# Fused attention and expert layers on one Trainium2 core: K and V of a batch loaded in two transfers each over all 128 partitions, q(0), q(1) and the gate requested by ACT, and K's fifth column turned at a step's end

## The chip, the cores and the metric

The kernel runs on one core of one Trainium2 chip. The metric is the device time of one execution in microseconds (us); lower is better. Times of the kernel before are three runs on one chip; the trace shown further down is one further execution of the same kernel, taken by the hardware profiler. Engines are named as the profile names them: PE is the matrix engine and PEld its weight loads, DVE the vector engine, ACT the scalar engine, POOL GpSimd, and SP the queue that issues most DMAs.

## The reference

Attention over K and V that are averaged in groups of eight rows, then a layer of eight experts with one expert for each token, then a layer with a squared ReLU. Only the attention is touched by the change.

```python
B, H, S, D = 4, 8, 576, 64
k_p = k.reshape(B, H, S // 8, 8, D).mean(axis=3)        # 72 rows for each head
v_p = v.reshape(B, H, S // 8, 8, D).mean(axis=3)
scores = matmul(q, k_p.transpose(0, 1, 3, 2)) / sqrt(D)
attn = softmax(scores)
x = matmul(attn, v_p)                                   # then (2304, 512): one row for each token
logits = x @ w_gate;  expert = argmax(logits);  gate = softmax(logits)[expert]
y[token] = gate * (relu(x @ w1[expert]) @ w2[expert])   # up to `capacity` tokens for each expert
out = (s * relu(y @ w_in) ** 2 + b) @ w_out
```

## The kernel before

The attention comes first and takes about the first 120 us; the experts (up to about 375 us) and the last layer follow, and both keep PE nearly full. The order of the work is written out by hand: each engine runs its instructions in the order in which the Python code emits them, and waits on semaphores where it needs another engine or a transfer.

The attention works on 20 tiles of up to 128 query rows, five for each of the four batches (four of 128 rows and one of 64), with all eight heads in a tile. Step i of the loop turns q of tile i+4 (`turn_q`: four transposes on PE into `tq`, and a copy to `qT` by ACT), makes the scores of tile i+3 (`scores`: PE products into `sc`, then on DVE the row maxima `mx` and the subtraction into `s`, then on ACT two exponentials, `e` and `s`), multiplies tile i by V (`values`: PE into `o`, then DVE into `xr` and the gate's logits `lg`), and turns the weights of tile i+2 (`turn_e`: PE into `te`, and a copy to `eT` by ACT). Tile i=1 gets its values ahead of step 0, so step 1 has none.

Four things have to be ready for a batch b. K is loaded (`load_k`) and its eight rows of a group are added up (`pool_steps`, three additions of 256, 128 and 64 columns for each head) into `kp`; `prep_k` turns `kp` on PE into the bank `misc` and moves it, scaled, into the block-diagonal `kbd`, which every score product of the batch reads. V is loaded (`load_v`), added up in the same way into `vp`, and `prep_v0` and `prep_v1` make `vx` from it. The additions are shared out between DVE and POOL.

K of a batch lies on 72 partitions (one for each pooled row), eight heads side by side, in two transfers of four heads. V of a batch lies on 128 partitions in five columns. A column p below four holds the pair of heads 2p and 2p+1: rows 0 to 71 are the even head's and rows 72 to 127 the first 56 of the odd head. The last 16 rows of the four odd heads stand in the fifth column, at partitions 16 to 31 of each group of 32. V needs six transfers: one of 72 partitions, one of 56, and four of 16.

SP issues all of these transfers and those of q in the order of the code. Eight completion counters are shared by the DMAs that SP and ACT issue, so that the ninth DMA waits until the first has landed, and so on. There is one buffer for K and one for V; q has four.

Of the kernel before, what the change touches and what calls it, by code (L numbers as in the profile page):

```python
# [7 lines left out]
F32 = mybir.dt.float32  # L8
# [4 lines left out]
ALU = mybir.AluOpType  # L13
# [5 lines left out]
B, H, S, D = 4, 8, 576, 64  # L19
# [3 lines left out]
POOL = 8  # L23
SP = S // POOL
P = 128
NB = 5
# [50 lines left out]
def attention(nc, tc, c, a, cap, capp, left, big, xd, run, hist, first, ps0):  # L77
# [3 lines left out]
    with ExitStack() as es:  # L81
# [6 lines left out]
        nc.vector.memset(wg, 0.0)  # L88
        kbd = [one.tile([P, 4, 2 * SP], F32, name=f"kbd{i}") for i in range(2)]
        vx = [one.tile([P, G, VW], F32, name=f"vx{i}") for i in range(2)]  # L90
        vraw = big.tile([P, NB, POOL, D], F32, name="vraw")
        nc.gpsimd.memset(vraw[:, 4], 0.0)
        for i in range(2):
            nc.vector.memset(kbd[i], 0.0)
            nc.gpsimd.tensor_scalar(out=vx[i][:, :, D], in0=c.mask, scalar1=float(POOL), scalar2=None, op0=ALU.mult)
# [26 lines left out]

        raw, sums = {}, {}

        def load_k(b):
            r = big.tile([SP, H, POOL, D], F32, name="kraw")
            src = a["k"][b].rearrange("h (n j) d -> n h j d", j=POOL)
            for i in range(2):
                nc.sync.dma_start(out=r[:, 4 * i:4 * i + 4], in_=src[:, 4 * i:4 * i + 4])
            raw["k", b] = r  # L130

        def load_v(b):
            src = a["v"][b].rearrange("(p w) (n j) d -> w n p j d", w=2, j=POOL)
            nc.sync.dma_start(out=vraw[0:SP, 0:4], in_=src[0])
            nc.sync.dma_start(out=vraw[SP:P, 0:4], in_=src[1, 0:P - SP])
            for p in range(4):
                nc.sync.dma_start(out=vraw[32 * p + 16:32 * p + 32, 4], in_=src[1, P - SP:, p])
            raw["v", b] = vraw

        def pool_steps(kv, b, h0, h1, eng):  # L140

            hs = slice(h0, h1)
            r = raw[kv, b][:, hs]
            if (kv, b) not in sums:
                sums[kv, b] = two.tile([SP, H, D] if kv == "k" else [P, NB, D], F32, name=kv + "p")
# [12 lines left out]
            yield  # L158
            for z in each(few[2]):
                eng.tensor_add(dst[:, z], r[:, z, 0], r[:, z, 1])  # L160
            yield

        def pool_all(kv, b, h0, h1, eng):
            for _ in pool_steps(kv, b, h0, h1, eng):
                pass

        def prep_k(b):
            tp = ps0.tile([P, 4, SP], F32, name="misc")
            for p in range(4):
                nc.tensor.transpose(tp[:, p], sums["k", b][:, 2 * p:2 * p + 2].rearrange("n h d -> n (h d)"), c.ident[:SP, :SP])  # L170
            for w in range(2):
                r = slice(D * w, D * w + D)
                dst = kbd[b % 2][r, :, SP * w:SP * w + SP]
                if b:
                    nc.scalar.mul(dst, tp[r], KSCALE)
                else:
                    nc.vector.tensor_scalar(out=dst, in0=tp[r], scalar1=KSCALE, scalar2=None, op0=ALU.mult)

        vts = {}

# [23 lines left out]
        N = len(tiles)  # L204
        qs, qts, ss, ets = {}, {}, {}, {}

        def load_q(i):
            if i < N:
                b, t = tiles[i]
                n = rows(t)  # L210
                qs[i] = two.tile([P, H, D], F32, name="q", bufs=4)
                nc.sync.dma_start(out=qs[i][:n], in_=a["q"][b, :, t * P:t * P + n].rearrange("h s d -> s h d"))

        def turn_q(i, bank="tq"):
            if i < N:
                n = rows(tiles[i][1])
                q = qs.pop(i)
                tq = ps1.tile([P, 2, 4, P], F32, name="te")[:, 0] if bank == "te" else ps0.tile([P, 4, P], F32, name="tq")
# [38 lines left out]
        def turn_e(i):  # L257
            if i < N:
                n = rows(tiles[i][1])
                s, e = ss.pop(i)  # L260
                te = ps1.tile([P, 2, 4, P], F32, name="te").rearrange("k j p s -> k (j p) s")
                for p in range(4):
                    nc.tensor.transpose(te[:, p, :n], s[:n, p, 0:P], c.ident[:n, :n])
                nc.tensor.transpose(te[:, 4, :n], e[:n].rearrange("s p k -> s (p k)"), c.ident[:n, :n])
                ets[i] = two.tile([P, NB, P], F32, name="eT", bufs=4)
                nc.scalar.copy(ets[i][:, :, :n], te[:, 0:NB, :n])
# [174 lines left out]
            else:  # L441
                nc.vector.tensor_copy(lists, n)

        load_k(0)
        load_gate()
        load_q(0)
        load_q(1)
        load_v(0)
        load_q(2)
        load_q(3)  # L450
        load_k(1)
        pool_all("k", 0, 0, 3, nc.vector)
        pool_all("k", 0, 3, 4, nc.gpsimd)
        pool_all("k", 0, 4, 7, nc.vector)
        pool_all("k", 0, 7, 8, nc.gpsimd)

        first.nc.sync.dma_start(out=first.idc.rearrange("(p n) o -> p (n o)", p=SUB), in_=big_ids)
        o = ps1.tile([P, 2, 512], F32, name="o")
        for _ in range(33):
            nc.tensor.transpose(o[:, 0, 0:P], c.ident, c.ident)  # L460
        turn_q(0)
        prep_k(0)
        turn_q(1, "te")
# [13 lines left out]
        turn_e(1)  # L477
        for i in (4, 5, 6, 7):
            load_q(i)
        load_v(1)  # L480
        pool_all("k", 1, 0, 5, nc.gpsimd)
        pool_all("k", 1, 5, H, nc.vector)
        dv = iter(())
        for i, (b, t) in enumerate(tiles):
            now[0] = i + 1
            if t == 1 and 0 < b < B - 1:
                prep_k(b + 1)
            if t == 3 and 0 < b < B - 1:
                prep_v0(b + 1)
            turn_q(i + 4)  # L490
            if i == 1:
                prep_k(1)
            scores(i + 3)
            if t == 4 and b < B - 1:
                prep_v1(b + 1)
# [7 lines left out]
            if i == 3:  # L503
                prep_v0(1)
            turn_e(i + 2)
            load_q(i + 8)
            if b >= B - 2:
                scale()
# [5 lines left out]
            if b + 1 < B:  # L514
                if t == (b == 0):
                    pool_all("v", b + 1, 0, SPLIT[b], nc.gpsimd)
                    dv = pool_steps("v", b + 1, SPLIT[b], NB, nc.vector)
                    next(dv)
                    if b:
                        next(dv)  # L520
                if i in (1, 4):
                    load_k(2 if i == 1 else 3)
                if t == 3 and b + 2 < B:
                    load_v(b + 2)
                if i in (2, 3):
                    pool_all("k", 2, 4 * i - 8, 4 * i - 4, nc.gpsimd)
                elif i == 6:
                    pool_all("k", 3, 0, 4, nc.gpsimd)
                    pool_all("k", 3, 4, 8, nc.gpsimd)
# [1125 lines left out]
```

## Time and profile before

| | |
|---|---|
| Time of three runs | 633.31, 635.12 and 637.03 us, median 635.12 us |
| The profiled execution | 635.53 us, of which 633.8 us lie between its first and last instruction |
| PE busy | 583.3 us (92% of the span) |
| DVE busy | 371.0 us (59%) |
| ACT busy | 249.4 us (39%) |
| POOL busy | 277.2 us (44%) |
| Moved by DMA | 86.12 MB, mean 136 GB/s |

All times in the trace count from its first instruction. Shares of the whole span say little here, since the attention and the two layers behind it have different limits; the attention is read from its own stretch.

### The profile page before, as it was taken

What the parts mean: (1) busy time and instruction counts of PE and PEld (TensorE: products, weight loads), DVE (VectorE), ACT (ScalarE), POOL (GpSimd) and SP (SyncE); (2) the same over time, 40 slices, a digit from 0 to 9 for tenths busy, and PEclk for the clock granted to TensorE, in tenths of its full rate; (3) what the DMA queues carried; (4) which work ended last, traced back from release to release, by engine and by line L of the source; (5) the groups of instructions that cost most, each with busy time, mean ns of one, the idle gap of its engine ahead of it and who ended that gap; (6) DMA issues with size and microseconds to landing.
All of it is one profiled execution on the core that took longest, in us unless ns stands there. A gap on an engine that the chain in (4) does not pass through costs nothing. (4 is left out here: it accounts for less than half of the span.)

```text
span 633.8 us, 11287 instructions
## 1 busy us (share of the span) xinstructions
PE 583.3 (92%) x4005; PEld 540.7 (85%) x4005; DVE 371.0 (59%) x901; ACT 249.4 (39%) x614; POOL 277.2 (44%) x462
## 2 busy tenths in 40 slices
PE   5788989699899969998899898999999999999995
PEld 5787878689899969998899778889899899899895
DVE  4687898977978976573758999713712022021050
ACT  1354654535456645435325635314115024033040
POOL 6557644715244805213207703406726336156051
PEclk8799999699899989999999998999999999999998
DMA  8999776636748895756677201017300100100000
GB/s 167 191 188 181 164 220 211 208 113 210 264 134 273 271 306 179 259 173 204 196 220 289 78 25 43 2 50 282 113 21 1 51 18 2 50 18 3 19 20 20
DMA packets 67951, 86.12 MB, mean 136 GB/s; under 512 B 24713, under 2 KB 40073, under 8 KB 67856
## 3 DMA queue, kind: packets, MB, share of 16 engines
q1 hardware_dynamic: 57168, 71.04, 38.1%
q10 hardware_dynamic: 8240, 7.14, 3.8%
q0 software_dynamic: 2448, 6.82, 3.4%
q8 instruction: 42, 0.69, 0.5%
q14 instruction: 53, 0.43, 0.2%
HBM read 68.09 MB, written 17.58 MB: 135 GB/s over the span
## 5 line engine op out<-in xcount | busy, mean ns | idle before, releaser
L1442 POOL TENSOR_TENSOR gl<-rt,gh 128x128 fp32r<-128x128 f32 x176 | 87.5, 519 | 84.0 <-ACT gh L1439 79.7
L1449 PE MATMUL bank<-wo,gh 128*128 128x512 f32 (+1 forms) x340 | 99.5, 376 | 0.2 <-DVE wo L1400 0.2
L936 POOL TENSOR_TENSOR w1l<-kraw,w1h 128x128 fp32r<-128x128 f32 x96 | 51.5, 569 | 51.9 <-ACT w1h L929 51.8
L1113 PE MATMUL bank<-hs,w2h 128*128 128x288 f32 (+1 forms) x308 | 68.5, 311 | 5.5 <-issue 5.1
L1449 PEld LDWEIGHTS bank<-wo,gh 128*128 128x128 f32 x340 | 62.0, 188 | 12.8 <-DVE wo L1400 0.5
L1449 PE MATMUL bank<-wo,gl 128*128 128x512 f32 (+1 forms) x170 | 63.8, 375 | 0.0
L1456 DVE SCALAR_TENSOR_TENSOR raw<-bank,sb,c_u 128x512 f32<-128x512 f32 (+1 forms) x14 | 10.0, 711 | 82.1 <-PE bank L1449 82.1
L1113 PEld LDWEIGHTS bank<-hs,w2h 128*128 128x128 f32 x308 | 50.7, 192 | 6.5 <-issue 5.9
L1424 ACT ACTIVATE rt<-tq 128x256 f32<-128x256 f32 (+1 forms) x26 | 9.5, 367 | 110.5 <-PE tq L1040 89.6
L1113 PE MATMUL bank<-hs,w2l 128*128 128x288 f32 (+1 forms) x148 | 44.9, 303 | 0.0
L1439 ACT CAST gh<-rt 128x256 fp32r<-128x256 f32 (+1 forms) x96 | 36.7, 383 | 17.4 <-DVE rt L1425 11.1
L944 POOL DMA_INDIRECT xg<-xd,u_idx x23 | 26.2, 1138 | 33.5 <-DVE r L290 13.9
L1457 POOL DMA_INDIRECT out_dram<-raw,it x12 | 12.5, 1040 | 63.2 <-DVE raw L1456 62.6
L1425 DVE SCALAR_TENSOR_TENSOR rt<-bank,rt 128x256 f32<-128x256 f32 (+1 forms) x53 | 21.2, 400 | 31.9 <-ACT rt L1424 31.8
L1449 PEld LDWEIGHTS bank<-wo,gl 128*128 128x128 f32 x170 | 31.9, 188 | 6.4
L1424 ACT ACTIVATE rt<-bank 128x256 f32<-128x256 f32 (+1 forms) x60 | 22.2, 371 | 30.1 <-PE bank L1040 27.5
L1040 PE MATMUL bank<-yhl,w2h 128*128 128x256 f32 x176 | 32.2, 284 | 1.1 <-DVE gl L1444 1.1
L1040 PE MATMUL bank<-yhl,w1h 128*128 128x256 f32 x176 | 31.0, 279 | 0.0
L230 PE MATMUL sc<-kbd,qT 128*128 128x144 f32 (+1 forms) x152 | 25.3, 314 | 5.7 <-DVE rmine L380 3.3
L967 PE MATMUL bank<-xs,w1h 128*128 128x288 f32 (+1 forms) x120 | 27.4, 315 | 2.0 <-DVE hs L970 2.0
L1425 DVE SCALAR_TENSOR_TENSOR rt<-tq,rt 128x256 f32<-128x256 f32 (+1 forms) x24 | 9.6, 400 | 32.9 <-ACT rt L1424 32.8
L1040 PEld LDWEIGHTS bank<-yhl,w2h 128*128 128x128 f32 x176 | 27.4, 192 | 1.2 <-DVE gl L1444 1.2
(495 smaller groups left out, 1691.9 us busy)
## 6 DMA issues: line engine op xcount, KB each, us to landing
kraw<-in_moe_w_dram SPq DMA_DIRECT2D x14, 1024.0 KB
vraw<-in_moe_w_dram SPq DMA_DIRECT2D x14, 1024.0 KB
c_raw<-in_moe_w_in_dram ACTq DMA_DIRECT2D x13, 512.0 KB
wo<-in_moe_w_out_dram SPq DMA_DIRECT2D x13, 512.0 KB
kraw<-in_k_dram SPq DMA_DIRECT2D x8, 576.0 KB
out_dram<-c_u SPq DMA_DIRECT2D x1, 4608.0 KB
q<-in_q_dram SPq DMA_DIRECT2D x16, 256.0 KB
xd<-xr SPq DMA_DIRECT2D x16, 256.0 KB
```

Of the source, the lines that this page charges most:

```text
L230: nc.tensor.matmul(sc[:n, p // 2, p % 2 * 144:p % 2 * 144 + 144], lhsT=q[:, p, :n], rhs=kbd[b % 2][:, p], start=True, stop=True)
L936: eng.tensor_sub(self.w1l[:, i, z], self.w1(i)[:, z], self.w1h[:, i, z])
L944: self.nc.gpsimd.indirect_dma_start(out=dst, out_offset=None, in_=self.xd[:have], in_offset=bass.IndirectOffsetOnAxis(ap=idx[:n], axis=0), ...
L967: self.nc.tensor.matmul(p, lhsT=l[:, f, k], rhs=r[k], start=n == 0, stop=n == 3 * KD - 1)
L1040: self.nc.tensor.matmul(p[:, :CU], lhsT=l[:, k], rhs=r[:, k], start=n == 0, stop=n == 3 * KD - 1)
L1113: nc.tensor.matmul(py[d][:, :v.n], lhsT=l[f][:, d * P:d * P + P], rhs=r[f], start=f == 0 and i == 0, stop=f == KF - 1 and i == 2)
L1424: nc.scalar.activation(r, p, AF.Relu)
L1425: nc.vector.scalar_tensor_tensor(out=p if inside else r, in0=p, scalar=0.0, in1=r, op0=ALU.max, op1=ALU.mult)
L1439: nc.scalar.copy(h[:, :n], r)
L1442: nc.gpsimd.tensor_sub(l[:, z:z + P], r[:, z:z + P], h[:, z:z + P])
L1449: nc.tensor.matmul(p[:, c], lhsT=g[:, j * P:j * P + P], rhs=wo[f][:, z, c], start=f == 0 and i == 0, stop=f == KF2 - 1 and i == 2)
L1457: i = nc.gpsimd.indirect_dma_start(out=dst, out_offset=bass.IndirectOffsetOnAxis(ap=ids, axis=0), in_=o[:, c], in_offset=None, bounds_chec ...
```

## The change

K gets V's layout: 128 partitions and five columns. `load` serves both and needs two transfers for a batch: one of 128 rows by four pairs of heads (for K of batch 0 two transfers of two pairs each), and one that fills the fifth column. The latter reads rows 112 to 143 of each pair, 32 rows for each of the four pairs; 16 of these 32 stand in the columns before already and are masked out or skipped later. So a batch of K or V is 640 packets of 2 KB in place of 576. The last addition of K writes each sum twice, side by side, so that one transpose of a column gives both halves of `kbd`.

`prep_k` becomes `prep_k0`, which turns the first four columns and makes two moves, and `prep_k1`, which turns the fifth column and makes a third move of 64 partitions by 4 by 16. For batches 1 to 3 `prep_k0` stands where `prep_k` stood, and `prep_k1` stands at the end of the same step, behind `turn_e`. In the first batch the additions of K are all on DVE, and one of the moves of `prep_k0` is on ACT.

ACT asks for q(0) and q(1) ahead of the gate's five small transfers; before, SP asked for q(0) and q(1) behind K. K of batch 1 is requested at the same place of SP's queue as before.

```diff
-        vraw = big.tile([P, NB, POOL, D], F32, name="vraw")
-        nc.gpsimd.memset(vraw[:, 4], 0.0)
+        raws = [big.tile([P, NB, POOL, D], F32, name=kv + "raw") for kv in "kv"]
...
+        def load(kv, b, few=4):
+            r = raws[kv == "v"]
+            src = a[kv][b].rearrange("(p w) (n j) d -> (w n) p j d", w=2, j=POOL)
+            for p in range(0, 4, few):
+                nc.sync.dma_start(out=r[:, p:p + few], in_=src[0:P, p:p + few])
+            src = src[2 * SP - 32:].rearrange("k p j d -> p k (j d)")
+            nc.sync.dma_start(out=r[:, 4].rearrange("r j d -> r (j d)"), in_=src)
+            raw[kv, b] = r
...
             for z in each(few[2]):
-                eng.tensor_add(dst[:, z], r[:, z, 0], r[:, z, 1])
+                x = (r[:, z, j] for j in range(2))
+                if kv == "k":
+                    x = (y.unsqueeze(2).to_broadcast([P, y.shape[1], 2, D]) for y in x)
+                eng.tensor_add(dst[:, z], *x)
...
+        def prep_k0(b):
+            t = ps0.tile([P, 4, P], F32, name="misc")
             for p in range(4):
+                turn_k(b, t[:, p], p)
+            move_k(kbd[b % 2][0:D, :, 0:SP], t[0:D, :, 0:SP], nc.scalar if b else nc.vector)
+            move_k(kbd[b % 2][D:P, :, SP:P], t[D:P, :, SP:P], nc.scalar)
+
+        def prep_k1(b):
+            t = ps0.tile([P, 512], F32, name="misc")[:, 0:P] if b else ps1.tile([P, 2, 512], F32, name="te")[:, 0, 0:P]
+            turn_k(b, t, 4)
+            move_k(kbd[b % 2][D:P, :, P:], t[D:P].rearrange("r (p n) -> r p n", p=4)[:, :, 16:], nc.scalar if b else nc.vector)
...
-        load_k(0)
+        load("k", 0, 2)
+        for i in range(2):
+            load_q(i, nc.scalar)
         load_gate()
-        load_q(0)
-        load_q(1)
-        load_v(0)
+        load("v", 0)
...
-        load_k(1)
-        pool_all("k", 0, 0, 3, nc.vector)
-        pool_all("k", 0, 3, 4, nc.gpsimd)
-        pool_all("k", 0, 4, 7, nc.vector)
-        pool_all("k", 0, 7, 8, nc.gpsimd)
+        pool_all("k", 0, 0, 2, nc.vector)
+        pool_all("k", 0, 2, NB, nc.vector)
+        load("k", 1)
...
-        pool_all("k", 1, 0, 5, nc.gpsimd)
-        pool_all("k", 1, 5, H, nc.vector)
+        pool_all("k", 1, 0, 3, nc.gpsimd)
+        pool_all("k", 1, 3, NB, nc.vector)
...
             turn_e(i + 2)
+            if t == 1 and b < B - 1:
+                prep_k1(b + 1)
```

The first place is the head of SP's queue, up to K of batch 1 (`72x4x512` is 72 partitions by four pieces of 512 numbers). Before:

```order
L129 DMA kraw<-in_k_dram 72x4x512 x2
L212 DMA q<-in_q_dram 128x8x64 x2
L134 DMA vraw<-in_v_dram 72x4x512
L135 DMA vraw<-in_v_dram 56x4x512
L137 DMA vraw<-in_v_dram 16x512 x4
L212 DMA q<-in_q_dram 128x8x64 x2
L129 DMA kraw<-in_k_dram 72x4x512 x2
```

And of the change:

```order
L128 DMA kraw<-in_k_dram 128x2x512 x2
L130 DMA kraw<-in_k_dram 128x1x512
L128 DMA vraw<-in_v_dram 128x4x512
L130 DMA vraw<-in_v_dram 128x1x512
L217 DMA q<-in_q_dram 128x8x64 x2
L128 DMA kraw<-in_k_dram 128x4x512
L130 DMA kraw<-in_k_dram 128x1x512
```

V of batch 0 stands directly behind K, the queue is seven requests shorter up to the same point, and q(0) and q(1) are gone from it; they stand first in ACT's queue.

The second place is ACT in steps 1 and 2, where `kbd` of batch 1 is filled (`kbd_164`; the 64-row exponentials are those of tile 4). Before:

```order
L222 COPY qT<-tq 128x512
L175 ACTIVATE kbd_164<-misc 64x4x72 x2
L246 ACTIVATE e<-s 64x128
L247 ACTIVATE s<-s 64x4x128
L266 COPY eT<-te 128x640
L222 COPY qT<-tq 128x512
```

And of the change:

```order
L227 COPY qT<-tq 128x512
L168 ACTIVATE kbd_164<-misc 64x4x72
L168 ACTIVATE kbd_164<-misc 64x4x56
L251 ACTIVATE e<-s 64x128
L252 ACTIVATE s<-s 64x4x128
L271 COPY eT<-te 128x640
L168 ACTIVATE kbd_164<-misc 64x4x16
L227 COPY qT<-tq 128x512
```

The last piece of `kbd` has moved behind the two exponentials of tile 4 and the copy of `eT`.

The third place is PE at the same point, from the turning of K to the first score product that reads `kbd_164` (tile 5). Before:

```order
L170 MATMUL misc<-ident,kp 128x72 x4
L230 MATMUL sc<-kbd_163,qT 64x144 x4
L263 MATMUL te<-ident,s 128x128 x4
L264 MATMUL te<-ident,e 128x128
L220 MATMUL tq<-ident,q 128x128 x4
L230 MATMUL sc<-kbd_164,qT 128x144 x4
```

And of the change:

```order
L164 MATMUL misc<-ident,kp 128x128 x4
L235 MATMUL sc<-kbd_163,qT 64x144 x4
L268 MATMUL te<-ident,s 128x128 x4
L269 MATMUL te<-ident,e 128x128
L164 MATMUL misc<-ident,kp 128x128
L225 MATMUL tq<-ident,q 128x128 x4
L235 MATMUL sc<-kbd_164,qT 128x144 x4
```

One transpose more stands between `te` and `tq`, and the four others are 128 columns wide in place of 72.

## Rows read from the trace of the kernel before

**Rows 1.** Stretches: length, engines' busy time, granted clock, DMA share, GB/s.
```profile
0.00:5.00 5.00, 3.45 (x18) 3.45 (x19) 1.30 (x6) 0.29 (x1) 4.12 (x30) 1.00 0.44 101
5.00:10.00 5.00, 1.80 (x17) 1.56 (x15) 2.47 (x4) 1.00 (x1) 3.31 (x10) 1.00 1.03 192
50.00:60.00 10.00, 9.27 (x78) 8.26 (x77) 6.35 (x22) 4.39 (x10) 7.38 (x12) 1.00 0.96 177
90.00:100.00 10.00, 9.36 (x76) 8.29 (x76) 9.44 (x37) 6.13 (x13) 0.00 (x0) 1.00 0.49 159
```

**Rows 2.** Waits, 0 to 110 us: total us, times, longest us.
```profile
DVE vraw L154 <- DMA vraw<-in_v_dram: 6.0, 3, 2.6
```

**Rows 3.** SP's DMA queue at 33:34, 66.5:67.5, 146:150 us: packets, MB, share of 16 engines.
```profile
q1 hardware_dynamic: 116, 0.22, 98.6%
...
q1 hardware_dynamic: 854, 0.25, 110.0%
...
q1 hardware_dynamic: 801, 1.60, 105.3%
```

**Rows 4.** Timeline, batch 0's K to first scores: start, us, instruction, idle before.
```profile
10.52 0.95 DVE L154 TENSOR_TENSOR kraw<-kraw 72x768 f32<-72x768 f32 x1 [0.71 <-DMA kraw<-in_k_dram]
...
12.51 0.49 DVE L160 TENSOR_TENSOR kp<-kraw 72x192 f32<-72x192 f32 x1
...
13.66 0.92 DVE L177 TENSOR_SCALAR kbd<-misc 64x288 f32<-64x288 f32 x2 [0.65 <-PE misc L170]
...
14.73 2.26 PE L230 MATMUL o<-kbd,qT 128*128 128x144 f32 x8 [0.26 <-DVE kbd L177]
...
17.82 0.76 DVE L242 TENSOR_TENSOR s<-o,mx 128x576 f32<-128x576 f32 x1
```

**Rows 5.** Timeline of DVE: additions of V of batch 0 and K of batch 1.
```profile
20.14 1.13 DVE L154 TENSOR_TENSOR vraw<-vraw 128x768 f32<-128x768 f32 x1 [1.57 <-DMA vraw<-in_v_dram]
...
21.31 0.96 DVE L157 TENSOR_TENSOR vraw<-vraw 128x384 f32<-128x384 f32 x1
...
22.30 0.49 DVE L160 TENSOR_TENSOR vp<-vraw 128x192 f32<-128x192 f32 x1
...
31.61 1.18 DVE L154 TENSOR_TENSOR kraw<-kraw 72x768 f32<-72x768 f32 x1
...
32.83 0.56 DVE L157 TENSOR_TENSOR kraw<-kraw 72x384 f32<-72x384 f32 x1
```

**Rows 6.** Timeline, steps 1 and 2, where the scores first read batch 1's K.
```profile
37.54 0.75 DVE L242 TENSOR_TENSOR s<-sc,mx 64x576 f32<-64x576 f32 x1
...
38.32 0.31 ACT L246 ACTIVATE e<-s 64x128 f32<-64x128 f32 x1 [0.23 <-DVE s L242]
38.44 1.22 PE L230 MATMUL sc<-kbd,qT 128*128 128x144 f32 x8 [0.28 <-DVE s L242]
...
39.32 0.69 ACT L266 COPY eT<-te 128x640 f32<-128x640 f32 x1
...
40.11 0.84 DVE L154 TENSOR_TENSOR vraw<-vraw 128x512 f32<-128x512 f32 x1 [1.83 <-DMA vraw<-in_v_dram]
...
40.88 0.74 DVE L236 TENSOR_REDUCE mx<-sc 128x8 f32<-128x576 f32 x1
```

**Rows 7.** Timeline, V of batch 2: its request by SP, its addition, DVE behind it.
```profile
44.68 2.77 SPq L134 DMA_DIRECT2D vraw<-in_v_dram  x1
...
59.27 0.59 DVE L154 TENSOR_TENSOR vraw<-vraw 128x256 f32<-128x256 f32 x1 [2.65 <-DMA vraw<-in_v_dram]
...
61.42 0.75 DVE L242 TENSOR_TENSOR s<-sc,mx 64x576 f32<-64x576 f32 x1
...
66.39 0.75 DVE L236 TENSOR_REDUCE mx<-sc 128x8 f32<-128x576 f32 x1
```

**Rows 8.** Tile kraw, 0 to 100 us: durations in ns (min/median/max), first and last start.
```profile
L154 POOL TENSOR_TENSOR kraw<-kraw x23: 718/723/1492, 7.3 to 71.8; 72x256 f32<-72x256 f32 x23
```

**Rows 9.** Waits, 107 to 400 us: the expert weights' first use.
```profile
ACT w1h L929 <- DMA kraw<-in_moe_w_dram: 0.8, 1, 0.8
```

More of the change, by code (lines that the diff above doesn't have):

```diff
@@ L123, in attention @@
         raw, sums = {}, {}
[L125 to L138, printed above, removed]
+        def load(kv, b, few=4):
[6 more added lines that the diff above has]
+            raw[kv, b] = r
         def pool_steps(kv, b, h0, h1, eng):
@@ L144, in pool_steps @@
             if (kv, b) not in sums:
-                sums[kv, b] = two.tile([SP, H, D] if kv == "k" else [P, NB, D], F32, name=kv + "p")
+                sums[kv, b] = two.tile([P, NB, 2, D] if kv == "k" else [P, NB, D], F32, name=kv + "p")
             dst = sums[kv, b][:, hs]
@@ L165, in pool_all, with turn_k, move_k @@
                 pass
-        def prep_k(b):
-            tp = ps0.tile([P, 4, SP], F32, name="misc")
-            for p in range(4):
[L170 to L177, printed above, removed]
+        def turn_k(b, t, p):
+            nc.tensor.transpose(t, sums["k", b][:, p].rearrange("r w d -> r (w d)"), c.ident)
+        def move_k(dst, t, eng):
+            if eng is nc.scalar:
+                eng.mul(dst, t, KSCALE)
+            else:
+                eng.tensor_scalar(out=dst, in0=t, scalar1=KSCALE, scalar2=None, op0=ALU.mult)
+        def prep_k0(b):
+            t = ps0.tile([P, 4, P], F32, name="misc")
+            for p in range(4):
+                turn_k(b, t[:, p], p)
[5 more added lines that the diff above has]
+            move_k(kbd[b % 2][D:P, :, P:], t[D:P].rearrange("r (p n) -> r p n", p=4)[:, :, 16:], nc.scalar if b else nc.vector)
         vts = {}
@@ L205, in attention, with load_q @@
         qs, qts, ss, ets = {}, {}, {}, {}
-        def load_q(i):
+        def load_q(i, eng=nc.sync):
             if i < N:
@@ L211, in load_q, with turn_q @@
                 qs[i] = two.tile([P, H, D], F32, name="q", bufs=4)
-                nc.sync.dma_start(out=qs[i][:n], in_=a["q"][b, :, t * P:t * P + n].rearrange("h s d -> s h d"))
-        def turn_q(i, bank="tq"):
+                eng.dma_start(out=qs[i][:n], in_=a["q"][b, :, t * P:t * P + n].rearrange("h s d -> s h d"))
+        def turn_q(i):
             if i < N:
@@ L217, in turn_q @@
                 q = qs.pop(i)
-                tq = ps1.tile([P, 2, 4, P], F32, name="te")[:, 0] if bank == "te" else ps0.tile([P, 4, P], F32, name="tq")
+                tq = ps0.tile([P, 4, P], F32, name="tq")
                 for p in range(4):
@@ L461, in attention @@
         turn_q(0)
-        prep_k(0)
-        turn_q(1, "te")
+        prep_k0(0)
+        prep_k1(0)
+        turn_q(1)
         sc = products(0, "o"), products(1)
@@ L479, in attention @@
             load_q(i)
-        load_v(1)
-        pool_all("k", 1, 0, 5, nc.gpsimd)
-        pool_all("k", 1, 5, H, nc.vector)
+        load("v", 1)
+        pool_all("k", 1, 0, 3, nc.gpsimd)
+        pool_all("k", 1, 3, NB, nc.vector)
         dv = iter(())
@@ L486, in attention @@
             if t == 1 and 0 < b < B - 1:
-                prep_k(b + 1)
+                prep_k0(b + 1)
             if t == 3 and 0 < b < B - 1:
@@ L491, in attention @@
             if i == 1:
-                prep_k(1)
+                prep_k0(1)
             scores(i + 3)
@@ L521, in attention @@
                 if i in (1, 4):
-                    load_k(2 if i == 1 else 3)
+                    load("k", 2 if i == 1 else 3)
                 if t == 3 and b + 2 < B:
-                    load_v(b + 2)
+                    load("v", b + 2)
                 if i in (2, 3):
-                    pool_all("k", 2, 4 * i - 8, 4 * i - 4, nc.gpsimd)
+                    pool_all("k", 2, 3 * i - 6, 2 * i - 1, nc.gpsimd)
                 elif i == 6:
-                    pool_all("k", 3, 0, 4, nc.gpsimd)
-                    pool_all("k", 3, 4, 8, nc.gpsimd)
+                    pool_all("k", 3, 0, NB, nc.gpsimd)
             step()
```

## The prediction

> **What bounds the kernel now.** The table of stretches comes first. Up to 60 us the 16 DMA engines are as good as full, at 177 to 192 GB/s, while DVE is busy 6.35 of 10 us in the sixth stretch; from 90 us on the DMA share is half, and DVE with 9.44 of 10 is the fullest engine [rows 1]. So the attention has two limits: first the loads, then DVE and PE in turn.
>
> The waits say what the loads cost DVE: 6.0 us in three waits for V [rows 2]. The timeline shows them one by one: 1.57 for V of batch 0, 1.83 for batch 1, 2.65 for batch 2 [rows 5 to 7]. DVE works in order, and the row maxima of the next tile stand behind each wait. POOL waits for V too, but nothing on DVE waits for POOL there, so I price DVE alone.
>
> Last, are the loads slow because the DMA engines are at their limit, or because of how they are cut? The queue's lines at three places tell [rows 3]. From 33 to 34 us 116 packets, nearly all of 2 KB, fill 98.6% of the engines: 136 ns each (0.986 x 16,000 / 116). From 146 to 150 us, when expert weights are loaded to 128 partitions, 801 packets of the same size take 84 ns each (1.053 x 64,000 / 801) and move 400 GB/s. From 66.5 to 67.5 us, nearly all q, 854 packets take 20.6 ns. A packet of K or V is thus 1.6 times as dear as a packet of a 128-partition load.
>
> **Part by part.** A batch of K or V becomes 640 packets in place of 576, 11% more. At 84 ns that is 54 us of engine time in place of 78 at 136 ns, so the bytes added weigh less than the rate gained, if the rate is gained. No row shows a 128-partition load of K. Its bounds are the two rates above.
>
> *Start.* In the first batch, K's second half reaches DVE at 10.52 and the first products start at 14.73, 4.21 us later [rows 4]. Now K and the two q are 1.84 MB (1.31 + 0.52). At the old rates, 101 and 192 GB/s [rows 1], 1.47 MB are in by 10.0 and the rest by 11.9. At 400 GB/s, counted from 2.4 us (5 - 0.505/0.192), they are in by 7.0. I take 10.5, no change. It lies nearer the slow end because a quarter of the bytes is q in small packets, and because the transfer of the fifth column reads from four pairs only and comes last. Behind the landing: DVE adds three columns in 0.95 + 0.56 + 0.56 = 2.07 (0.95 is the row of 768 numbers [rows 4], 0.56 that of 384 [rows 5]), where it took 2.48 (10.52 to 13.00). Then 0.66 to turn (13.00 to 13.66), 0.26 for one transpose more (an estimate: a quarter of the 1.0 that four took), 0.46 for the move that stays on DVE (half of 0.92; the other goes to ACT beside it), 0.24 for the fifth column's move and 0.15 to the products: 3.84, which is **-0.4**. Bounds with the landing: -3.9 to +1.0. ACT's gate requests now stand behind q and wait on the shared counters, with ACT's first copy behind them; they are over when q(1) has landed, before `kbd` is ready, so I cost them at nothing. If q(1) came after 12 us they would show.
>
> *V of batch 0.* It is requested directly behind K, ahead of where K's load used to end. The subtraction of tile 0 ends at 18.58, 17.82 + 0.76 [rows 4], and V came at 20.14. The 1.57 goes. DVE's three additions took 2.65 (20.14 to 22.79), while POOL added its own columns of the same load; the same sizes without that are 0.95 + 0.56 + about 0.37 = 1.88. POOL will now be done earlier. I take **-2.2** of 2.3; bounds 0 to -2.3. PE is idle there and only follows.
>
> *K of batch 1 on DVE.* Three heads of 448 numbers become two columns of 512 (the last sum is written twice). By a line through 384 (0.56) and 768 (0.95) this is 0.69 + 0.43 + 0.43 = 1.55, against about 2.15 from 31.61 on (1.18, 0.56 and a third) [rows 5]. The maxima of tile 3 stand right behind: **-0.6**, bounds 0 to -0.7.
>
> *The fifth column at the step's end.* In step 1, DVE ends the subtraction of tile 4 at 38.29, and PE starts the products of tile 5 at 38.44, because `kbd` is ready. Now the last piece of `kbd` waits in ACT's queue behind `e` (38.32), `s` and the copy of `eT`, which ends at 40.01; with its own 0.2 or so the products start at about 40.25, end at 41.47, and the maxima start then, 0.6 later than the 40.88 of before [rows 6]. `values` of tile 2 queues behind these products on PE, and DVE waits for it once more. So V of batch 1 arrives in time and gains nothing: its 1.83 is replaced by a wait for PE. **+0.9**, bounds +0.3 to +1.5. In the two later batches the same thing happens, but DVE has work of its own between the subtraction and the next maxima: in step 7 from 62.17 to 66.39, 4.2 us [rows 7], and the delayed products need about 3.2. So nothing there; with that cover gone it would be up to 1.8 each.
>
> *V of batch 2.* SP asks at 44.68, and DVE needs it at 56.62, when it starts the wait of 2.65 that ends at 59.27 [rows 7]. Before it, the terms above have moved DVE 2.3 us ahead, so 12 us are left in both cases. 640 packets at 84 ns on 16 engines are 3.4 us, at 136 ns 5.4, and the q beside it 1.3 each. It should be there. I take **-2.3**, bounds 0 to -2.65. Next in line is DVE itself.
>
> *POOL.* For K of batches 2 and 3 the 8 + 8 first additions of 0.72 us [rows 8] become 5 + 5. POOL is not on the path; it slows DVE where both add, so **-0.2**, bounds 0 to -0.7. PE's wider transposes cost some 0.3 us in each batch, hidden behind DVE.
>
> The sum is -0.4 - 2.2 - 0.6 + 0.9 - 2.3 - 0.2 = -4.8. Loads of expert weights follow by program order and are waited for only 0.8 us at first use [rows 9], so an earlier attention should bring all behind it forward. The profiled execution took 635.5, the median is 635.1: **630.3 us**.
>
> **The rivals.** *The fifth columns crowd a few DMA engines (slower).* If the transfer whose source is four pairs runs on four engines, these get 64 packets of a load and the others 32. At the slow price of 136 ns, K of batch 0 and two q take them 64 x 0.136 + 128 x 0.0206 = 11.3 us, so K lands at 13.7 in place of 10.5: +3.2 at the start. V of batch 0, 8.7 us later on the same engines, comes at 22.4, or 1 us after the subtraction: half of that gain is left, -1.2. Batch 2's wait is cut to 1.5 us: -1.1. With -0.6, +0.9, -0.4 and a stall of POOL's share of V behind the same engines (+1.5), the sum is +2.3, and 637.4; with the fifth of K of batch 1 late as well it passes 638.3. It decides from a landing of K after about 14 us. Against it: at 84 ns the same four engines are through with K and q by 10.4, which is my landing. [...] No view of this trace names the engine of a packet.
>
> *The loads get faster, and new waits eat it (no change).* The delayed products cost 1.8 in batches 2 and 3 also, because PE, not DVE, is late in the step: +3.6, so 633.9. For it: PE was busy 9.36 of 10 us from 90 on [rows 1]. Against it: the 4.2 us of DVE work in step 7.
>
> *The rate is not gained (no change).* If a packet stays at 136 ns because many q packets share the engines, 11% more bytes come at the old rate, all three waits stay, and -0.4 - 0.6 + 0.9 leaves 635.
>
> *All of it and a faster start.* With K in by 8 us the start gains 2.5 more: 627.8.
>
> **How the numbers follow.** Chances: the forecast 0.48 (628.5 to 632.5), the faster start 0.10, new waits 0.20, rate not gained 0.11, crowded engines 0.11. A difference of 0.5%, 3.2 us, is about what a measurement here can tell from none. Faster by more, below 631.9: nearly all of the first two and a little of the third, 0.57. Slower, above 638.3: most of the crowded engines, 0.09. Within: 0.34. The range 627.0 to 637.0 leaves out about 0.05 below and 0.12 above.
>
> **What would show it.** In the changed trace: packets of 2 KB at 350 GB/s or more in the first 60 us, and a DMA share well under 1.0 by 50 us; DVE's waits for V gone at batches 0 and 2; the products of tile 5 starting about 2 us behind the subtraction of tile 4, behind an ACT instruction on `kbd`; first products at 14.3 or so. The prediction is wrong if the products of tile 0 start after 16 us, if a wait for V over 1 us remains in batch 2, or if products in steps 7 and 12 make DVE wait more than 1 us each. The time from the attention's end to the end should be as before within 1 us.

## The result, and the profile after

The changed kernel takes 639.88 us (median of nine runs, 636.62 to 644.48), the kernel before 635.25 (nine runs, 633.31 to 637.03). The ratio is 1.0076, with a 95% interval of 1.0054 to 1.0099: slower, where 630.3 was forecast, and above the range given. The profiled execution took 639.99 us, its span is 638.1, 4.3 longer than before.

Two things happened, in two stages. The attention, forecast 4.8 us shorter, ended level. And some 4 us were lost where the change touches no line, in the middle of the experts.

**The loads.** The table of stretches of the changed kernel answers to [rows 1]:

```profile
5.00:10.00 5.00, 3.67 (x25) 3.44 (x23) 1.54 (x3) 0.00 (x0) 0.49 (x6) 1.00 1.12 277
20.00:30.00 10.00, 8.08 (x59) 7.05 (x57) 7.82 (x14) 4.60 (x10) 4.38 (x6) 0.97 0.91 211
```

From 5 to 10 us the DMA engines move 277 GB/s where they moved 192. SP's queue at 33:34 us (packets, MB, share of 16 engines; it answers to the first of [rows 3]):

```profile
q1 hardware_dynamic: 198, 0.41, 104.0%
```

These are 84 ns a packet (1.040 x 16,000 / 198) where it was 136, the fast one of the prediction's two prices: the rate was gained. (Up to K of batch 1 SP's queue has 9 requests in place of 14; it is five shorter, not seven.) The waits of the changed kernel (0 to 110 us; total, times, longest) show that this is not what DVE feels:

```profile
PE sc L235 <- ACT kbd L168: 6.7, 3, 4.0
...
DVE vraw L147 <- DMA vraw<-in_v_dram: 4.9, 2, 2.9
```

DVE still waits 4.9 us for V, where it was 6.0 [rows 2]; only batch 0's wait is gone. The timeline of the start answers to [rows 4]:

```profile
13.48 0.96 DVE L147 TENSOR_TENSOR kraw<-kraw 128x768 f32<-128x768 f32 x1 [6.76 <-DMA kraw<-in_k_dram]
...
15.19 0.60 ACTq L120 DMA_DIRECT2D wg<-in_moe_w_gate_dram  x1
...
15.82 1.28 ACT L227 ACT_TABLE_LOAD   x1 [15.82 <-DVE rev L69]
...
16.88 0.23 DVE L170 TENSOR_SCALAR kbd<-te 64x64 f32<-64x64 f32 x1
...
18.66 2.13 PE L235 MATMUL o<-kbd,qT 128*128 128x144 f32 x8
```

K is complete at 13.4 in place of 10.5, and the first products start 3.9 us late. The records of the completion counters tell why. Each transfer raises its counter as its parts land; the reports of K's three transfers of batch 0 in the changed kernel, in us:

```
first two pairs    16 reports   4.25 ...  5.08
other two pairs    16 reports   6.70 ...  7.59
fifth column        4 reports  12.63 13.27 13.29 13.38
```

The fifth column reports four landings in place of sixteen and comes 5.8 us after the rest. I read a report as one engine's share; no view names the engine of a packet. Behind the landing stands a second delay: ACT's last gate request waited until 15.19 for the counter of q(1), whose last report came at 15.16; behind it stand a table load of 1.28 us, the copy of qT(0) and ACT's share of `kbd`.

V of batch 0 (DVE; it answers to [rows 5]) is added without a wait, as forecast:

```profile
21.62 0.76 DVE L247 TENSOR_TENSOR s<-o,mx 128x576 f32<-128x576 f32 x1
22.30 0.95 DVE L147 TENSOR_TENSOR vraw<-vraw 128x768 f32<-128x768 f32 x1
23.28 0.56 DVE L150 TENSOR_TENSOR vraw<-vraw 128x384 f32<-128x384 f32 x1
23.87 0.36 DVE L156 TENSOR_TENSOR vp<-vraw 128x192 f32<-128x192 f32 x1
```

But its fifth column reported its four landings only from 19.35 to 19.67. The subtraction of tile 0 ends at 22.38 here, 3.8 us later than before, and that is why nothing waits.

In step 1 and at V of batch 2 (they answer to [rows 6, 7]) DVE waits:

```profile
36.65 0.75 DVE L247 TENSOR_TENSOR s<-sc,mx 64x576 f32<-64x576 f32 x1
...
39.42 1.25 PE L235 MATMUL sc<-kbd,qT 128*128 128x144 f32 x8 [1.55 <-ACT kbd L168]
...
40.33 0.69 DVE L147 TENSOR_TENSOR vraw<-vraw 128x512 f32<-128x512 f32 x1 [2.93 <-DMA vraw<-in_v_dram]
...
58.55 0.75 DVE L147 TENSOR_TENSOR vraw<-vraw 128x256 f32<-128x256 f32 x1 [2.01 <-DMA vraw<-in_v_dram]
```

Both waits end with the fifth column: V of batch 1 had its first four columns in by 35.58 and the fifth by four reports from 39.97 to 40.23; V of batch 2 by 54.80 and 58.52.

DVE's row `xr` near 107 us, in the attention's last steps, starts at 106.65; before it was 106.83. So the attention is level.

**The experts.** PE's timeline shows where the time went. Before:

```profile
295.92 1.22 PE L1248 MATMUL bank<-rt,vraw 128*128 128x144 f32 x8 [1.90 <-ACT w1h L1089]
296.97 0.44 PE L1233 MATMUL tq<-ident,xg 96*128 96x96 f32 x2
297.34 1.53 PE L1248 MATMUL bank<-rt,vraw 128*128 128x144 f32 x8
...
302.01 4.19 PE L1248 MATMUL bank<-hs,vraw 128*128 128x144 f32 x32
```

And of the changed kernel, whose lines are five higher:

```profile
294.46 1.22 PE L1253 MATMUL bank<-rt,vraw 128*128 128x144 f32 x8 [1.80 <-ACT c_u L881]
295.52 0.44 PE L1238 MATMUL tq<-ident,xg 96*128 96x96 f32 x2
295.88 0.39 PE L1253 MATMUL bank<-rt,vraw 128*128 128x144 f32 x1
298.59 2.05 PE L1253 MATMUL bank<-rt,vraw 128*128 128x144 f32 x7 [2.31 <-issue]
...
301.00 2.29 PE L1253 MATMUL bank<-rt,vraw 128*128 128x144 f32 x8
...
306.29 4.71 PE L1253 MATMUL bank<-hs,vraw 128*128 128x144 f32 x32
```

It enters this stretch 1.5 us ahead. Then it stops in the middle of a group of eight equal products, and "issue" says that it waits for nothing that the profile shows. The groups behind it take 2.29 us in place of 1.25. The stretches 295:300 and 300:305 of the changed kernel show the granted clock (the number before the last two):

```profile
295.00:300.00 5.00, 2.69 (x15) 2.28 (x14) 0.31 (x1) 1.17 (x3) 3.18 (x3) 0.71 1.01 377
300.00:305.00 5.00, 5.00 (x20) 4.21 (x20) 0.62 (x2) 0.00 (x0) 0.00 (x0) 0.50 0.14 45
```

In the stretch behind the stop the clock is granted at 0.50; in the kernel before it is 1.00 from 295 to 310 us. The products on `hs` start at 306.29, before at 302.01: 1.5 ahead has become 4.3 behind. Where the last layer's products begin, 2.9 are left (392.26 for 389.38), and 1.4 come on again at the very end, in POOL's drain behind its last store (from the store's end at 631.26 to the span's end at 638.1; before 628.32 to 633.8). What arrives during the stop is in the DMA view of 296.1 to 297.2 us:

```profile
q1 hardware_dynamic: 207, 0.42, 99.3%
q8 instruction: 1, 0.02, 5.4%
```

One packet of the queue that the profile calls instruction, amid transfers that fill the engines. The page has this row for the whole span:

```profile
q8 instruction: 42, 0.69, 0.5%
```

That is 16 KB a packet, and they start some 20 us apart while PE works evenly. I read them as PE's code; no view says what a packet holds. Before the stop PE had jumped: the branch at the end of an `If`, behind which it skips the `Else`, ended at 294.0. A stop for "issue" behind an earlier branch, at 229 to 240 us, stands in all fourteen traces (3.9 to 5.5 us; 5.11 before, 4.33 here), so such stops are nothing new in this kernel; the one near 296 us is.

### The profile page after: what moved, and what is told of

It is laid out like the page before. It is cut to its first block, busy times and chain, and to the rows that moved or that the text cites. A ratio compares the mean times of both kernels' runs of the same rounds, so it can differ in the third digit from the quotient of the medians.

```text
span 638.1 us, 11258 instructions
## 1 busy us (share of the span) xinstructions
PE 584.9 (92%) x4009; PEld 543.2 (85%) x4009; DVE 367.5 (58%) x901; ACT 251.6 (39%) x618; POOL 262.3 (41%) x443
## 5 line engine op out<-in xcount | busy, mean ns | idle before, releaser
L235 PE MATMUL sc<-kbd,qT 128*128 128x144 f32 (+1 forms) x152 | 23.9, 302 | 6.7 <-ACT kbd L168 6.7
L1118 PEld LDWEIGHTS bank<-hs,w2l 128*128 128x128 f32 x148 | 28.5, 193 | 0.0
```

The lines of the kernel that those rows point to most:

```text
L235: nc.tensor.matmul(sc[:n, p // 2, p % 2 * 144:p % 2 * 144 + 144], lhsT=q[:, p, :n], rhs=kbd[b % 2][:, p], start=True, stop=True)
L1118: nc.tensor.matmul(py[d][:, :v.n], lhsT=l[f][:, d * P:d * P + P], rhs=r[f], start=f == 0 and i == 0, stop=f == KF - 1 and i == 2)
```

## The experiments

Each stands against the kernel before, run beside it on the same chip. In the expectations, "places" counts PE's instructions ahead of the experts, a product as two (its weights and itself) and a separate wait as one, in the built program: 2035 before, 2048 in the change.

### The changed kernel once more

> The changed kernel once more, for a second trace of it. First theory (crowding): the fifth columns' transfers run on four engines and K of batch 0 and V of batches 1 and 2 land late; K's fifth column lands between 12 and 14 us and the first products start between 18 and 19 us, as in the first trace of the changed kernel (13.38 and 18.66). Rival (later stage): in that first trace the attention was level with before at its end (DVE 0.9 us ahead at 127 us and PE 1.7 ahead at 236), and 4 us and more were lost only between 290 and 311 us, where PE stood idle for 2.31 us and then ran at half clock. If that is what makes the changed kernel slow, a second trace shows a loss of 4 us or more in that stretch again; if it was chance, PE's start of the last layer's transposes (392.3 us in the first trace, 389.4 in before) comes at another time, and the gap to before lies elsewhere.

639.02 us, one execution. First products at 17.71, V of batch 1 waited for 2.7 us, V of batch 2 not at all; and the same stop:

```profile
300.08 1.33 PE L1253 MATMUL bank<-rt,vraw 128*128 128x144 f32 x4 [3.18 <-issue]
```

The start was a little better than expected (17.71 for 18 to 19), the late loss was no chance of one execution.

### Fifth columns cut by pair

```diff
-            nc.sync.dma_start(out=r[:, 4].rearrange("r j d -> r (j d)"), in_=src)
+            for p in range(4):
+                nc.sync.dma_start(out=r[32 * p:32 * p + 32, 4].rearrange("r j d -> r (j d)"), in_=src[p])
```

> The changed kernel with the transfer of a fifth column cut into four, one for each pair (32 rows on 32 partitions each); bytes, packets and layout unchanged. Crowding: each of the four has 16 increments spread over all engines, K of batch 0 is complete by 8.5 to 10.5 us in place of 13.4, q(1) comes with it, the first products start at 13 to 15 us in place of 18.66, the waits for V in batches 1 and 2 (2.9 and 2.0 us) shrink below 1 us; the time falls to 633 to 637 us. Later stage: the attention gets faster, the time does not follow, 638 to 643. Against both: SP issues nine more transfers up to V of batch 1 and the eight counters go round faster, so a request of SP can wait longer; if that eats the gain, SP's requests for V show it.

637.75 us, ratio 1.0039 (1.0011 to 1.0067), between the two ranges. K was complete at 11.59 and the first products started at 15.59, both later than crowding expected, and no wait of DVE for V is left over 1 us. DVE was 4.1 us ahead of before at tile 3, but 0.4 at 107 us; the stop near 302 us is there (3.60). So each theory describes its own stage, and neither the time.

### The fifth column of K turned early

```diff
                 prep_k0(b + 1)
+                prep_k1(b + 1)
...
-            if t == 1 and b < B - 1:
-                prep_k1(b + 1)
```

> The changed kernel with the fifth column of K turned right behind the first four in batches 1 to 3 (for batch 0 nothing changes). The third piece of kbd then stands ahead of the exponentials in ACT's queue, and PE's wait of 1.8 us before the products of tile 5, and those of 0.9 or less in the later batches, go. Crowding: V of batch 1 still lands at 40.2 us, DVE waits for it anyway, so 0 to -1 us: 639 to 640. If the order within the step is the cause of the loss: -2 to -4 us, 636 to 638. Later stage: no change beyond 1 us.

643.02 us, ratio 1.0107 (1.0069 to 1.0145), where neither theory expected a loss. The interval overlaps that of the change, but in this trace DVE is 5.5 us behind before at 107 us. The waits name a new one:

```profile
PE misc L164 <- ACT kbd L168: 6.3, 3, 2.5
```

There is one bank `misc`; the fifth column's transpose waits until ACT has moved the first four out, and what stands behind it on PE waits too.

### Both

> Both edits at once: fifth columns cut by pair, and turned right behind the first four. Crowding, with the order as a second bound: the gains add up, since V of batch 1 is there in time and the products of tile 5 no longer wait; 631 to 635 us. Later stage: 638 to 643 in spite of an attention that ends 3 us or more earlier.

638.79 us, ratio 1.0048 (1.0020 to 1.0075). DVE was 3.0 us ahead of before at 79.7 us and 0.3 at 90, with 6.4 us of that same wait for the bank; and the stop (3.18). Neither theory alone gives this.

### The warm-up of before, seven transposes longer

```diff
-        for _ in range(33):
+        for _ in range(40):
             nc.tensor.transpose(o[:, 0, 0:P], c.ident, c.ident)
```

> The kernel before, with 40 warm-up transposes on PE in place of 33 at the very start, where PE is idle anyway; nothing else. That moves all later PE instructions 14 places back in PE's instruction stream (the changed kernel: 13 places by the same count, the last run 4). Theory of places: in all four traces of changed kernels PE stands idle for 2.3 to 3.6 us at the same spot near 296 us, where the queue that brings PE's code (16 KB at a time) is just delivering the next piece, and half clock follows; where the pieces end is set by the number of PE instructions ahead. Then this kernel shows the same idle time and the same loss of 4 to 6 us between 296 and 306 us, and takes 638 to 641 us with an attention as before. Rival (requests): the code comes late because SP's request for 1 MB of expert weights now goes out 0.8 us sooner after the last store than before (5.5 against 6.4 us) and fills the DMA engines; the place in the stream is unchanged in its effect, and this kernel takes 634 to 637.

640.62 us, ratio 1.0074 (1.0043 to 1.0104). Seven transposes in PE's idle start cost the kernel before as much as the whole change. In its trace 1.8 us of that were lost in the attention, which was not expected, and 5.6 more between there and the last layer. Its PE timeline and the stretch in which it starts again:

```profile
297.78 1.22 PE L1248 MATMUL bank<-rt,vraw 128*128 128x144 f32 x8 [1.94 <-ACT w1h L1089]
298.84 0.44 PE L1233 MATMUL tq<-ident,xg 96*128 96x96 f32 x2
303.28 2.08 PE L1248 MATMUL bank<-rt,vraw 128*128 128x144 f32 x8 [4.01 <-issue]
```
```profile
300.00:305.00 5.00, 1.72 (x8) 1.72 (x8) 0.00 (x0) 0.00 (x0) 2.20 (x2) 0.57 0.77 277
```

### The warm-up of the change, seven shorter

The same line of the changed kernel, 26 for 33.

> The changed kernel with 26 warm-up transposes in place of 33: all later PE instructions stand one place ahead of those of before in place of 13 behind. [...] Rival (requests): the idle time stays, 638 to 641. Crowding (the fifth columns' transfers make the loss): 638 to 641 as well, since they are unchanged.

635.76 us, ratio 0.9987 (0.9951 to 1.0022): level with before, and within the 633 to 636 us that the theory of places gave for an idle time near 296 us that is gone or under 1 us. No stop, and the granted clock is 1.00 in each stretch from 290 to 310:

```profile
298.22 0.44 PE L1238 MATMUL tq<-ident,xg 96*128 96x96 f32 x2
298.59 1.25 PE L1253 MATMUL bank<-rt,vraw 128*128 128x144 f32 x8
```

The theory of places stands as far as the place goes; that a piece of code ends there is not shown. One more reading makes the place firmer. In the trace of the changed kernel 11 products, each with its weight load, lie between the jump and the stop, besides six semaphore instructions that stand there in all of them: 22 instructions, at 13 places back. In all six traces that stop there, instructions and places add up to 35: 22 in the three at 13 back, 21 at 14 back (ten products and eleven loads), and 31 in the two at 4 back (15 products and 16 loads), as in e2_k1_early:

```profile
301.69 0.88 PE L1253 MATMUL bank<-rt,vraw 128*128 128x144 f32 x5
305.19 0.53 PE L1253 MATMUL bank<-rt,vraw 128*128 128x144 f32 x3 [2.61 <-issue]
```

So PE stops at one fixed place of its instruction stream, whichever product stands there.

This trace's attention was 0.9 us behind before, so the fifth columns as the change has them bring nothing at a good place either.

### Cut, and turned between products and exponentials

```diff
-        def scores(i):
+        def scores(i, fifth=0):
             if i < N:
                 sc = products(i)
+                if fifth:
+                    prep_k1(fifth)
                 mx = maxima(i, sc)
...
-            scores(i + 3)
+            scores(i + 3, b + 1 if t == 1 and b < B - 1 else 0)
```

The first kernel has the cut and 28 warm-up transposes.

> Fifth columns cut by pair, and the fifth column of K turned between a tile's products and its exponentials (PE: behind the products that run in the meantime, so that the bank is free; ACT: ahead of the exponentials), with 28 warm-up transposes, so that the later PE instructions stand one place ahead of those of before. The run with both edits lost 3 us at 80 to 90 us because PE waited 2.3 us for the bank, and the run with the cut alone lost 2 us there to PE's wait for the third piece of kbd; here neither is left. Expected of the attention: PE's last products 2 to 3.5 us ahead of before at 107 us. Theory of places: 630 to 634 us. Rival (requests): 636 to 640, with the loss near 296 us again.

630.18 us, ratio 0.9925 (0.9890 to 0.9959). DVE and PE are 6.5 us ahead of before at 107 us, more than I expected; DVE never waits for V, and the longest wait for the bank is 1.4.

> The same with 53 warm-up transposes: the later PE instructions stand 49 places behind those of before. By the traces the end of a piece of code then moves from some 43 instructions behind PE's jump near 295 us to just ahead of it, so that PE has a whole piece to run. Theory of places: no idle time of over 1 us near 296 us, 629 to 634 us, unless another jump (228, 312, 597 us) now meets the end of a piece; that would show there. Rival (requests): 636 to 640.

628.96 us, ratio 0.9888 (0.9842 to 0.9934), no stop near 296 us, stops of 1.35 to 1.47 at 310 to 313 (1.52 in before). The two intervals overlap, so the places 49 back are not shown to be better than one ahead.

### The warm-up of before, 26 longer

The line of the diff above, 59 for 33.

> The kernel before with 59 warm-up transposes in place of 33: its later PE instructions stand 52 places further back, nearly as in the run with 53 warm-ups (49). Theory of places: how far back they stand is not good or bad by its amount; the end of a piece of code now falls ahead of PE's jump near 295 us, as in that run, so there is no idle time of over 1 us there, and the time is 632 to 636 us. If instead every place further back costs time, this kernel takes 640 us or more, as with 40 warm-ups. Rival: the long warm-up itself (PE busy to about 6 us in place of 4, and the clock with it) is what helped the run with 53; then products of tiles 0 and 1 run faster here and this kernel is 2 us or more ahead of before by 30 us.

634.55 us, ratio 0.9977 (0.9953 to 1.0002). 52 places back costs nothing where 14 cost 0.74%. At 28.5 us DVE was 0.4 behind before, so the longer warm-up did not help by itself. (The trace is of the slowest execution, 639.76; it lost 3.4 us in the attention and has no stop near 296 us.)

### The order without the cut

The diff of the order on the changed kernel, with 28 warm-up transposes.

> The changed kernel with its fifth columns in one transfer each, as in the change, but turned between products and exponentials, and with 28 warm-up transposes, so that the later PE instructions stand where those of the run e4_between_28 stood: the two differ in the cut of the fifth columns alone. Crowding: K's fifth column lands at 12.5 to 13.5 us by four increments, the first products start 2.5 to 4 us after those of before, DVE still waits 2 us or more for V of batch 1 and 1 to 3 us for V of batch 2, and the attention ends within 1.5 us of before: 633 to 637 us, 4 us or more behind e4_between_28. Rival: the order in the step was what held the attention up, and four engines are enough: 629 to 632, within 1.5 us of e4_between_28.

634.86 us, ratio 0.9975 (0.9950 to 1.0000). K's fifth column landed at 13.31 by four reports, the first products started 3.4 us after those of before, and DVE waited 3.04 us for V of batch 1 and 0.34 for V of batch 2. The latter is shorter and the attention better (2.9 us ahead of before at 107 us) than crowding expected.

### The cut without the order

The diff of the cut, with 26 warm-up transposes.

> The changed kernel with its fifth columns cut by pair, the fifth column of K turned at the step's end as in the change, and 26 warm-up transposes, so that the later PE instructions stand one place ahead of those of before. With a3_changed_26 (neither), e6_order_28 (the order alone) and e4_between_28 (both) this makes a table of two by two at one place in the code. In the trace of the cut with 33 warm-ups the attention was 2.2 us ahead of before at 80 us and lost 1.8 of it at 87 us, where PE waited 2.5 us for the third piece of kbd at the step's end. Expected if cut and order need each other: 633 to 636 us, a ratio to before of 0.995 to 1.000, with that wait again. If the cut alone were enough: 629 to 632, as e4_between_28.

633.77 us, ratio 0.9989 (0.9955 to 1.0023). Its trace is of its fastest execution (631.26), so the ratio decides; in that trace DVE is 4.1 us ahead of before at 107 us. PE's waits for ACT's third piece of `kbd` are there:

```profile
PE sc L236 <- ACT kbd L169: 3.9, 3, 1.5
```

At one place ahead the table is: neither 0.9987, cut 0.9989, order 0.9975, both 0.9925. Only both together are clear of before. But their interval (up to 0.9959) just meets those of the cut (from 0.9955) and of the order (from 0.9950), and in the traces DVE is 0.9 us behind at 107 us with neither, 4.1 ahead with the cut, 2.9 with the order and 6.5 with both, which looks rather like a sum. That cut and order need each other is not shown.

### The gate's requests on SP

```diff
-        load_gate()
         load("v", 0)
+        load_gate()
...
-                nc.scalar.dma_start(out=wg[D * q:D * q + D, ci, 2 * q:2 * q + 2], in_=wv[ci, q])
+                nc.sync.dma_start(out=wg[D * q:D * q + D, ci, 2 * q:2 * q + 2], in_=wv[ci, q])
```

> The run e5_between_53 with the gate's five requests moved from ACT to SP, behind V of batch 0. There the last two pieces of K's fifth column were requested only at 9.1 and 9.4 us, since the eight counters were taken by the gate's requests and they had to wait for q(1); now K and the two q take the eight counters by themselves. Expected if the start is held by that: K complete by 8 to 9.5 us, first products at 12 to 13.5 us (15.7 there), and 1 to 3 us less in all: 626 to 628. If the next wait takes it (V of batch 0, K of batch 1 behind the gate's requests on SP): 628 to 630, no change.

629.62 us, ratio 0.9891 (0.9861 to 0.9921). K was complete at 10.31, later than expected, the first products started at 13.99 in place of 15.72, and there is no gain in all: the lead of 6.2 us at 28.5 us was 2.3 at 37.5, and DVE waited for K of batch 1 (1.07) and V of batch 1 (1.03). The next wait took it.

## Why the prediction was wrong

**The step that failed first** is "an earlier attention should bring all behind it forward", and with it "The time from the attention's end to the end should be as before within 1 us". I took it that code which the change does not touch runs as before. It does not: PE's later instructions stand 13 places further back, and at 4, 13 and 14 places back PE stops for 2.3 to 4.0 us at one spot and its granted clock is 0.50 to 0.66 in the stretch of 5 us in or behind which it stops, while at 1 ahead, 0, 49 and 52 back it does not stop there over 1 us. The warm-up alone moves this both ways (1.0074 for before, 0.9987 for the change). In the first trace the whole loss against before lies behind the attention.

What happens at this place? In each of the six traces PE stops 21 to 31 instructions behind a jump, for 2.31 to 4.01 us, and the granted clock is then 0.50 to 0.66. The queue that the profile calls instruction moves 16 KB a packet (0.69 MB in 42), and one of its packets starts at 296.19 in the changed kernel, 0.1 us before PE stops (296.27 to 298.59). That this packet is PE's next code and that the fixed place is the end of a piece of it is how I read it; no view shows where a piece ends, and no run shows that PE waits for the packet.

Why this spot? In the kernel before, the packet of that queue starts at 296.07, 0.7 us after PE's jump ended, with the DMA engines idle; in the changed one at 296.19, 2.2 us after it, behind 1 MB of weights that SP requested at 293.35. At 1 ahead and 0 it is 0.7 us in all five traces, in the nine others 2.2 to 3.5. SP's request moves with the places too: 6.2 to 6.4 us after SP's last store of `yt` at 1 ahead and 0, 5.4 to 5.6 at 4, 13 and 14 back, 4.7 to 5.2 at 49 and 52 back. At 49 back (e5_between_53) the next such packet came 3.2 us after the jump, behind the weights, and PE did not stop. So a late packet alone did no harm there: if it is PE's code, the end of the piece that PE runs must be near as well. Whether a near end alone would, with the weights out of the way, these runs don't tell, nor why the request moves.

**Start: forecast -0.4, measured +3.9.** The failed step is the landing "unchanged at 10.5": it came at 13.38, where the rival of the crowded engines worked out 13.7. That the transfer of the fifth column runs on four engines no run shows. What the traces show are the reports: 4 by 128 reported four times, and cut into 32 by 32 (e4_between_28) the last piece reported sixteen times, from 11.12 to 11.40. I gave this rival 0.11 because at the fast price even four engines would do (10.4); I should have asked what else would lie on them. DVE's three additions took 2.08, 2.07 forecast. That ACT's gate requests cost nothing failed too: q(1) came at 15.16, past the 12 us that the prediction named, DVE's share of `kbd` was ready at 17.1, and the products started at 18.66.

**V of batch 0: forecast -2.2, met by luck.** DVE's maxima were 3.8 us late at tile 0 and 1.4 at tile 1: the wait is gone and the additions took 1.87. But V was complete only at 19.67, by a transfer that reported four times as well. Had the start kept its time, the subtraction would have ended near 18.2, and most of the old wait of 1.57 would have stayed. **K of batch 1: -0.6, right:** the maxima were 0.4 us ahead of before at tile 2 and 1.0 at tile 3.

**Not in the sum: the clock.** Before, PE's granted clock from 20 to 30 us was 0.66, in the change 0.97. The products of tile 2, before and then changed:

```profile
26.38 2.13 PE L230 MATMUL sc<-kbd,qT 128*128 128x144 f32 x8
```
```profile
26.86 1.25 PE L235 MATMUL sc<-kbd,qT 128*128 128x144 f32 x8
```

That is how maxima 1.4 us late at tile 1 were 0.4 ahead at tile 2, as I read it; in a3_changed_26, where the clock stayed low until 26.65, this step gained 1.1 in place of 1.8. I had no term for it.

**The fifth column at the step's end: forecast +0.9, measured +1.0, half by luck.** The products of tile 5 started 2.0 us after the subtraction, as forecast. But "V of batch 1 arrives in time" failed: 2.93, 2.7 and 1.4 us of waiting in three traces, so V held DVE as long as PE did. With V there (e1_fifth_by_pair), the order holds the step: DVE's lead fell from 4.0 at tile 4 to 2.3 at tile 5, while with the order as well (e4_between_28) it went from 4.2 to 4.7. In steps 7 and 12 the forecast held in the change: PE waited 4.00 and 1.11 us for the third piece of `kbd`, and DVE for no product. With the cut (e1_fifth_by_pair) PE waited 2.47 in step 12, and DVE's lead of 2.2 us at 80 us was 0.4 behind it.

**V of batch 2: forecast -2.3, measured -0.6** (2.65 to 2.01), and no wait in two other traces of the same attention. **POOL: -0.2**, too small to be seen.

So the attention's sum was -0.2 in place of -4.8, and the loss lies where the forecast's own rival had put it, at fifth columns that land late (13.38 for K of batch 0, 58.52 for V of batch 2), milder in the sum than I made it (+2.3); that crowded engines are the cause is a reading. That this rival's 637.4, or 638.3 and more, lies nearest to the measured 639.88 is luck: its loss was to come in the attention, and the time was lost behind it. The -4.8 was there to be had: with cut, order and a good place the kernel runs at 0.9925 and 0.9888.

## What to carry to other kernels

Look at how many landings a transfer reports: here one of 4 by 128 pieces reported four and came 5.8 us after its neighbours, and the same bytes cut into 32 by 32 reported sixteen. Ask too what else waits on the same counters. A change that adds or takes away a few instructions moves all the code behind it (here PE's by 13 places): where a kernel jumps and PE stops for "issue" in the middle of a group, change the count of some harmless instructions first, before and after, and only then judge the change. Two improvements that can't be told from nothing one by one may still gain 0.7% together; measure the pair before you drop either.

## What was not expected of the hardware

PE stops of up to 4.01 us at one fixed place of its instruction stream, about when one 16 KB packet of the queue called instruction arrives, followed by a stretch whose granted clock was 0.50 to 0.66; the time of the whole kernel depends on the number of PE instructions ahead by 0.74% between 0 and 14 places. The transfer that reported four landings seems to have delayed a neighbour as well: q(1), requested before the fifth column, had twelve of its sixteen reports in by 8.9 us and the last at 15.16.

POOL seems to do the same at the end. Its drain, in the changed kernel and then in before (ns shortest, median, longest; first and last start):

```profile
L1656 POOLq DRAIN  x3: 51/106/3154, 634.1 to 637.8; - x3
```
```profile
L1651 POOLq DRAIN  x3: 51/102/4326, 628.7 to 633.5; - x3
```

It starts 2.9 us behind the end of the last store, before 0.3, also at a jump, and costs 1.1 to 1.4 us at the end of all eleven traces with the change's POOL code (19 or 24 instructions shorter) and not in the two of before with a longer warm-up. That this is POOL's code is argued, not shown.
